# Six value products in one step, expert conversions behind the exp, and a later start of the second batch's scores

## The chip, the cores and the metric

The kernel runs on one core of a Trainium2 chip. The metric is the device time in microseconds of one execution. Before the change the median of three runs is 1456.61 us (1449.06 to 1458.63).

## The reference

The program is an attention block with mixed heads, followed by a bilinear expert layer; everything is float32 (the expert weights arrive as float64 and are rounded on the chip).

```python
# q, k, v: (8, 12, 448, 64), w_pre and w_post: (12, 12)
scores = np.matmul(q, k.transpose(0, 1, 3, 2)) / 8
scores = np.einsum('bhij,hg->bgij', scores, w_pre)
attn = np.exp(scores - np.max(scores, axis=-1, keepdims=True))
attn = attn / (np.sum(attn, axis=-1, keepdims=True) + 1e-09)
attn = np.einsum('bhij,hg->bgij', attn, w_post)
x = np.matmul(attn, v)             # regrouped to (3584, 768)
# w1, w2: (768, 1024), w3: (1024, 1024), w_out: (1024, 768)
out = ((x @ w1) * (x @ w2) @ w3) @ w_out
```

## The kernel before

The scores of a batch are cut into 45 tiles of ten query rows. The main loop in `run` has one **step** n per tile (8 x 45, and six more), and works on tiles in sets m of two. An even step 2m fetches rows of raw scores for a later set, takes the row maxima of set m on DVE (`largest`, L226), and its exp on ACT (`exp`, L234). The odd step 2m+1 scales the second mixing matrix by the sums (`scale`, L243 to L246), multiplies the set before with it on PE (`post`, L259), and mixes the heads of the next set's scores (`mix`, L219). The mix writes the two banks that the exp reads, so it waits for the exp of the set before. Everything is written in program order; each engine, and SP, which issues all DMAs, works through its own instructions in that order.

Around this, the steps carry other work:

- **Scores.** `qk` (L173) makes one unit of raw scores, copies it out of score banks 0 and 1 on ACT (L178, L179), and the next step stores it to DRAM. Lists `qks` and `loads` say in which step a unit is made and its `kq` pair is loaded (six steps ahead). The first batch's units stand in steps 0 to 14.
- **Value products.** After each group of 15 tiles `av` (L300) multiplies six pairs of heads with v, three into one bank. Three pairs are done in an odd step, the other three two steps later, all in bank 0. A copy on ACT (L321, for the first two batches followed by a subtraction on DVE, L322) or a copy and a store (L307) empties it. With a batch's last group the next batch's six v tiles are asked for (`load_v`, L285). The first six are loaded in steps 6 to 11.
- **Conversions.** The float64 expert weights are brought in as words (L100), squared on ACT (L106), put together on DVE in four operations (L116 to L120), and cut into a high part (ACT, L125) and a low part (POOL, L126). `converting` asks for words two conversions ahead. Forty of them (`fold_pieces`) feed the product of w3 and w_out (`folding`, L359, up to step 47); then 32 (`unit_pieces`) make the weights of the experts, which are also stored (L424). One is made in a step at most, and none in a step that has value products.
- **Experts.** The matrix products of the expert layer are handed out as single matmuls by `advance`, so many per step as `shares` works out: it gives more to steps with less other work (a value product counts 5.1, an odd step 9.3, a score unit 3.7).

`self.later`, `self.ends` and `self.soon` are lists of things to issue: at the start of the next step, when `do_ends` is called (after products, to empty banks), and after the maxima. `bank(i, ...)` first issues what still empties bank i.

## Time and profile before

| | |
|---|---|
| median of 3 runs | 1456.61 us |
| profiled execution, its own time | 1456.61 us |
| its span | 1454.8 us |
| PE busy | 1390.1 us, 96% of the span |
| ACT busy | 833.1 us, 57% |
| DVE busy | 739.0 us, 51% |
| POOL busy | 620.7 us, 43% |
| DMA | 416.86 MB, mean 287 GB/s |
| mean granted TensorE clock | 0.985 |

PE is the only engine that is busy nearly all the time. Its busy time includes matmuls that run at a lower granted clock. How busy the others are on the average says little, since the stretches of the program differ: at the start it converts and loads, from about 1280 us on it only runs experts. So the places where PE is idle are what is read, and for each the instruction it waited for.

### The profile page before, as it was taken

The page shows a single profiled execution, that of the slowest core. Times are in us where ns is not written, and L with a number is a line of the kernel's source. Part 1 is how long each engine was busy: PE and PEld are TensorE (multiplying, and loading weights), DVE is VectorE, ACT ScalarE, POOL GpSimd, SP SyncE. Part 2 cuts the span into 40 slices and gives each one's busy share as a digit, 9 for nine tenths or more (in the row PEclk, how much of TensorE's full clock was granted, in tenths as well). Part 3 has the DMA queues.
Part 4 walks back from the last instruction along what each step waited for, and adds up shares of the span by engine and source line. Part 5 has one row for each costly group of instructions (what it writes and reads, how often), then busy time and mean ns, then how long its engine had stood idle before and what let it go on. Part 6 is the DMA issues. An engine that isn't in the chain of part 4 may idle for free.

```text
span 1454.8 us, 45722 instructions
## 1 busy us (share of the span) xinstructions
PE 1390.1 (96%) x18684; PEld 1059.4 (73%) x18684; DVE 739.0 (51%) x1497; ACT 833.1 (57%) x1952; POOL 620.7 (43%) x754
## 2 busy tenths in 40 slices
PE   5789998999999989999999999999999999999998
PEld 2357785776677667776777777777776777899988
DVE  4867565767644544432344445334444447334563
ACT  3876665777756656665555656656655546422231
POOL 1333232444324434632244445444335446446683
PEclk7989998999999999999999999999999999999999
DMA  8998789999999999999989988799879766698875
GB/s 256 365 319 274 237 267 287 311 336 307 316 288 353 348 343 319 368 338 314 311 266 291 319 278 280 234 312 350 288 230 285 236 179 214 206 332 263 240 229 173
DMA packets 203760, 416.86 MB, mean 287 GB/s; under 512 B 20528, under 2 KB 120112, under 8 KB 203472
## 3 DMA queue, kind: packets, MB, share of 16 engines
q1 hardware_dynamic: 203552, 413.94, 87.2%
q8 instruction: 149, 2.44, 0.7%
q14 instruction: 59, 0.48, 0.1%
HBM read 279.77 MB, written 134.09 MB: 284 GB/s over the span
## 4 chain that ended last, share of the span: by engine, by line
PE 78%; DMA 13%; DVE 5%; ACT 3%; issue 1%; SPq 0%; POOL 0%; DVEq 0%; ACTq 0%; POOLq 0%
PE e L701 20%; PE psa L300 10%; PE pso L259 10%; PE psm L219 8%; PE psq L173 7%; PE psf L359 5%; PE eg L521 4%; PE e2o L701 4%; PE e1o L701 4%; PE e3o L701 4%; DMA s_d<-s 3%; PE eo L552 3%; DMA cs<-wo 3%; DMA r<-raw_d 2%; DMA wu<-w_d 2%; ACT e L234 1%
## 5 line engine op out<-in xcount | busy, mean ns | idle before, releaser
L246 POOL TENSOR_SCALAR w<-wpo,ri 128x60 f32<-128x60 f32 x360 | 180.7, 518 | 489.0 <-DVE ri L244 465.8
L226 DVE TENSOR_REDUCE mn<-psm 128x1 f32<-128x448 f32 x360 | 207.8, 619 | 317.0 <-PE psm L219 316.6
L701 PE MATMUL e<-eh,wu 128*128 128x448 f32 x1008 | 297.3, 372 | 6.3 <-DVE c L655 3.2
L273 ACT COPY mt<-pso 128x480 f32<-128x480 f32 x352 | 197.8, 621 | 177.3 <-PE pso L259 177.1
L234 ACT ACTIVATE e<-psm,mn 128x448 f32<-128x448 f32 x360 | 226.6, 642 | 9.6 <-DVE mn L226 9.6
L219 PE MATMUL psm<-r,wsc 60*64 60x448 f32 (+1 forms) x1440 | 197.9, 557 | 32.1 <-ACT e L234 19.9
L701 PEld LDWEIGHTS e<-eh,wu 128*128 128x128 f32 x1008 | 188.0, 188 | 52.5 <-issue 27.4
L259 PEld LDWEIGHTS pso<-w,e 60*64 60x64 f32 x10080 | 174.5, 134 | 50.0 <-issue 44.0
L259 PE MATMUL pso<-w,e 60*64 60x60 f32 x10080 | 198.6, 224 | 0.1
L701 PE MATMUL e<-el,wu 128*128 128x448 f32 x504 | 187.1, 371 | 0.0
L173 PE MATMUL psq<-kq 64*64 64x448 f32 x1176 | 159.5, 546 | 0.6 <-ACT st L178 0.6
L300 PE MATMUL psa<-mt,v 128*64 128x150 f32 (+1 forms) x2304 | 156.9, 293 | 1.9 <-ACT st L178 1.9
L300 PEld LDWEIGHTS psa<-mt,v 128*64 128x64 f32 x2304 | 143.6, 137 | 17.9 <-issue 6.3
L655 DVE TENSOR_TENSOR c<-c,e 128x448 f32<-128x448 f32 x168 | 101.8, 618 | 87.6 <-PE e L701 82.8
L178 ACT COPY st<-psq 128x448 f32<-128x448 f32 x162 | 86.4, 533 | 68.8 <-ACT mt L273 32.8
L521 PE MATMUL eg<-xh,wu 128*128 128x448 f32 x384 | 118.8, 380 | 4.8 <-DMA wu<-w_d 4.8
L640 POOL TENSOR_TENSOR el<-x,eh 128x448 fp32r<-128x448 f32 x90 | 104.2, 1176 | 34.8 <-ACT eh L639 34.8
L701 PEld LDWEIGHTS e<-el,wu 128*128 128x128 f32 x504 | 94.9, 188 | 22.4 <-issue 14.1
L243 DVE TENSOR_SCALAR sa<-sm 128x2 f32<-128x2 f32 x180 | 35.9, 200 | 129.6 <-ACT e L234 129.0
L173 PEld LDWEIGHTS psq<-kq 64*64 64x64 f32 x1176 | 62.2, 136 | 53.8 <-issue 29.8
L521 PEld LDWEIGHTS eg<-xh,wu 128*128 128x128 f32 x384 | 71.8, 190 | 38.1 <-issue 25.3
L179 ACT COPY st<-psq 128x448 f32<-128x448 f32 x162 | 87.7, 541 | 0.0
(99 smaller groups left out, 2011.5 us busy)
## 6 DMA issues: line engine op xcount, KB each, us to landing
r<-raw_d SPq DMA_DIRECT2D x344, 210.0 KB, 4.9
raw_d<-st SPq DMA_DIRECT2D x138, 448.0 KB, 5.4
wu<-w_d SPq DMA_DIRECT2D x104, 384.0 KB, 6.4
wu<-s_d SPq DMA_DIRECT2D x96, 384.0 KB, 4.8
wu<-w_d SPq DMA_DIRECT2D x51, 512.0 KB, 5.6
kq<-kq SPq DMA_DIRECT2D x42, 448.0 KB, 6.2
wu<-s_d SPq DMA_DIRECT2D x36, 512.0 KB, 4.9
x<-x_d SPq DMA_DIRECT2D x72, 224.0 KB, 6.3
```

The lines of the kernel that those rows point to most:

```text
L173: nc.tensor.matmul(ps[s][z * PP:(z + 1) * PP], t[rows, q:q + PP], t[rows, k:k + S], start=True, stop=True)
L219: nc.tensor.matmul(ps[s][c * PP:(c + 1) * PP, :S], self.wsc[k], r[k, c], start=True, stop=True)
L226: self.nc.vector.tensor_reduce(mn[:, s:s + 1], self.psm[m][s][:, :S], axis=AX.X, op=ALU.min)
L234: nc.scalar.activation(e, p[:, :S], AF.Exp, bias=mn[:, s:s + 1], scale=-1.0, accum_out=sm[:, s:s + 1])
L246: nc.gpsimd.tensor_scalar_mul(w2[:, s], self.wpo, ri[:, s:s + 1])
L259: nc.tensor.matmul(self.pso[c][z * PP:(z + 1) * PP, at:at + HK], e[k, j * PP:(j + 1) * PP], w2s[k, s], start=True, stop=True)
L273: self.nc.scalar.copy(dst.rearrange("p j g (s i) -> p j s g i", s=2), src)
L300: nc.tensor.matmul(self.psa[rows, g % 3, :W], v[:, j, rows], mt[:, j, 2 * g + s, :W], start=(j == 0), stop=(j == NJ - 1))
L521: nc.tensor.matmul(p, u[:, k % (K1 // 2), x], xs[y][:, k], start=(k == 0 and t == 0), stop=(k == K1 - 1 and t == 2))
L640: nc.gpsimd.tensor_tensor(lo, x, hi.bitcast(F32), op=ALU.subtract)
L655: nc.vector.tensor_tensor(a[out], a[to[0]], p, op=ALU.add)
L701: nc.tensor.matmul(p, w[:, k, x], ops[m, k][y], start=(k == 0 and t == 0), stop=(k == nk - 1 and t == 2))
```

## The change

Four things change. All six pairs of a group are multiplied in one step (pairs 0 to 2 into bank 0, 3 to 5 into bank 1), the step in which three were before. The expert conversions (`unit_pieces`) are issued later within a step: in an even step behind the exp, in an odd step at its end; they are now also made in the step that lost its three value products. The second batch's score units start at step 14 and not 11, one in 1.3 steps, and its kq loads with them; the first v loads stand in steps 11 to 16. And the experts of the first batch start one step earlier (`E_AT`).

```diff
--- before.py
+++ after.py
@@ -292,7 +292,7 @@
         nc, cols = self.nc, self.cols(a)
         W = cols.stop - cols.start
         if g % 3 == 0:
-            self.psa = self.bank(0, f"psa{b}_{a}_{g}")[:, :3 * GB * IB].rearrange("p (g i) -> p g i", g=3)
+            self.psa = self.bank(g // 3, f"psa{b}_{a}_{g}")[:, :3 * GB * IB].rearrange("p (g i) -> p g i", g=3)
         v, mt = self.vs[b, g], self.mt[b, a]
         for j in range(NJ):
             for s in range(2):
@@ -311,15 +311,15 @@
                 nc.sync.dma_start(dst, x)
                 self.x_made[b] += 1
 
-            self.ends.append((0, leave))
+            self.ends.append((g // 3, leave))
         elif g % 3 == 2:
             if b not in self.xs:
                 pool = self.xp[b % 2]
                 self.xs[b] = [pool.tile([128, K1, S], F32R, tag=f"x{t}", name=f"x{t}{b}") for t in "hl"]
             h, l = (x[:, g - 2:g + 1, cols] for x in self.xs[b])
             q = self.psa[:, :, :W]
-            self.ends.append((0, lambda: nc.scalar.copy(h, q)))
-            self.soon.append((0, lambda: nc.vector.tensor_tensor(l, q, h.bitcast(F32), op=ALU.subtract)))
+            self.ends.append((g // 3, lambda: nc.scalar.copy(h, q)))
+            self.soon.append((g // 3, lambda: nc.vector.tensor_tensor(l, q, h.bitcast(F32), op=ALU.subtract)))
         if a == NG - 1:
             self.later.append(self.load_v)
 
@@ -805,7 +805,7 @@
         for n, u in enumerate([(0, p, c) for c in (1, 2) for p in range(HP)] + [(0, p, 3) for p in range(1, HP, 2)]):
             qks[n] = [u]
         for b in range(1, B):
-            first, per = (11, 28 / 21) if b == 1 else ((b - 1) * NB - 6, NB / 21)
+            first, per = (14, 1.3) if b == 1 else ((b - 1) * NB - 6, NB / 21)
             units = [(b, p, c) for g in range(0, HP, 2) for p, c in [*itertools.product((g, g + 1), range(3)), (g + 1, 3)]]
             for i, (b, p, c) in enumerate(units):
                 n = int(first + i * per) | (b > 1)
@@ -815,11 +815,10 @@
         for b in range(B):
             for a in range(NG):
                 for g in range(HP):
-                    n = (b * NB + (a + 1) * GB + 3) | 1
-                    avs.setdefault(n if g < 3 else n + 2, []).append((b, a, g))
+                    avs.setdefault((b * NB + (a + 1) * GB + 3) | 1, []).append((b, a, g))
 
         N = B * NB
-        FOLD, SWITCH, E_AT = 18, NB + 5, NB + 8
+        FOLD, SWITCH, E_AT = 18, NB + 5, NB + 7
         PAIR, P_AT = 4 * NB + 7, 4 * NB + 15
         P_1 = 7 * 3 * (2 * K1 // 2 * KF // 2 + KF // 2 * K1 // 2)
         E_1, E_2 = 2 * KF * K1 * 3, K1 * KF * 3
@@ -926,7 +925,7 @@
             self.do_later()
             if n + 3 < HP:
                 others(n + 3)
-            elif HP <= n < 2 * HP:
+            elif HP <= n - 5 < 2 * HP:
                 self.load_v()
             for x in loads.get(n, []):
                 self.load_kq(*x)
@@ -948,7 +947,11 @@
             self.do_soon()
             if pieces:
                 next(pieces)
-            elif unit_pieces and not fold_pieces and not avs.get(n):
+
+            def convert():
+                nonlocal unit_pieces, n_pieces, third
+                if pieces or not unit_pieces or fold_pieces or avs.get(n):
+                    return
                 ahead = 1 if n < SWITCH else 2 * done // (3 * K1) + 4 + (done > 0)
                 if n_pieces < ahead:
                     n_pieces += 1
@@ -957,6 +960,7 @@
                     else:
                         next(unit_pieces)
                         third = True
+
             now = share.get(n, 0)
             if n < SWITCH:
 
@@ -966,8 +970,10 @@
 
             advance(now // 2)
             self.do_ends()
-            if not odd and m < SETS:
-                self.exp(m)
+            if not odd:
+                if m < SETS:
+                    self.exp(m)
+                convert()
             advance(now - now // 2)
             for x in avs.get(n, []):
                 self.av(*x)
@@ -979,6 +985,8 @@
             self.do_ends()
             for i, x in enumerate(qks.get(n, [])):
                 self.later.append(self.qk(*x, (6, 7) if i else (0, 1)))
+            if odd:
+                convert()
             if third:
                 next(unit_pieces)
```

How the order of instructions moves is seen at three places.

ACT, the program's steps 53 and 54 before. `cm` is a conversion's Square, `wu` its high part, `e` the exp, `mt` the copies behind `post`.

```order
L106 ACTIVATE cm_3275<-cs_3135 128x384
L273 COPY mt_0_2975<-pso_141 128x4x2x12x5
L273 COPY mt_0_2975<-pso_142 128x4x2x12x5
L125 CAST wu_3323<-cx_3255 128x3x128
L106 ACTIVATE cm_3335<-cs_3247 128x384
L234 ACTIVATE e_0_3349,sm_3348<-psm_0_3315,mn_3330 128x448
L234 ACTIVATE e_1_3351,sm_3348<-psm_1_3316,mn_3330 128x448
L125 CAST wu_3358<-cx_3281 128x3x128
L106 ACTIVATE cm_3373<-cs_3273 128x384
```

The same stretch with the change, from the copies of step 53 on:

```order
L273 COPY mt_0_2966<-pso_141 128x4x2x12x5
L273 COPY mt_0_2966<-pso_142 128x4x2x12x5
L106 ACTIVATE cm_3339<-cs_3239 128x384
L125 CAST wu_3347<-cx_3280 128x3x128
L234 ACTIVATE e_0_3363,sm_3362<-psm_0_3329,mn_3354 128x448
L234 ACTIVATE e_1_3365,sm_3362<-psm_1_3330,mn_3354 128x448
L106 ACTIVATE cm_3369<-cs_3272 128x384
L527 COPY ea_0_3381<-eg_0_0_3261 128x448
L125 CAST wu_3385<-cx_3345 128x3x128
```

In step 54 the Square (the second of the three before, the second of the two after) stood ahead of the two exps and now stands behind them. In step 53 it stood ahead of the copies behind `post` and now stands behind them.

SP, from step 5 to step 8 before. `cs` are a conversion's words, `raw_d<-st` a unit's scores, `r` the rows for the mix, `v` and `kq` the loads that move.

```order
L156 DMA kq_0_472<-kq 128x896
L100 DMA cs_474<-wo 128x768
L201 DMA r_541<-raw_d 60x2x448 x2
L187 DMA raw_d<-st_5_1_538 128x896
L285 DMA v_0_545<-v 128x512
L100 DMA cs_547<-wo 128x768
L187 DMA raw_d<-st_0_2_576 128x896
L285 DMA v_1_580<-v 128x512
L100 DMA cs_582<-wo 128x768
L201 DMA r_649<-raw_d 60x2x448 x2
L187 DMA raw_d<-st_1_2_646 128x896
L285 DMA v_2_653<-v 128x512
```

With the change:

```order
L100 DMA cs_472<-wo 128x768
L201 DMA r_539<-raw_d 60x2x448 x2
L187 DMA raw_d<-st_5_1_536 128x896
L100 DMA cs_543<-wo 128x768
L187 DMA raw_d<-st_0_2_572 128x896
L100 DMA cs_576<-wo 128x768
L201 DMA r_643<-raw_d 60x2x448 x2
L187 DMA raw_d<-st_1_2_640 128x896
L156 DMA kq_0_647<-kq 128x896
L100 DMA cs_649<-wo 128x768
L187 DMA raw_d<-st_2_2_678 128x896
L100 DMA cs_682<-wo 128x768
```

Three v loads and the kq load are gone from among the words, rows and stores here; the kq load now stands in step 8 and the v loads begin in step 11.

PE, the last group of the first batch, before: step 49, from the last fold matmuls to the first of `post`, and step 51, from the last scores on.

```order
L359 MATMUL psf_7_2940<-fo,fw_2678 128x384 x19
L300 MATMUL psa_2_0_3039<-mt_2_2168,v_0_545 64x148 x8
L300 MATMUL psa_2_0_3039<-mt_2_2168,v_1_580 64x148 x8
L300 MATMUL psa_2_0_3039<-mt_2_2168,v_2_653 64x148 x8
L259 MATMUL pso_141<-w_2922,e_0_2905 64x60
L259 MATMUL pso_142<-w_2922,e_0_2905 64x60
```

```order
L173 MATMUL psq_1_2_1_3103<-kq_1_2471 64x448
L300 MATMUL psa_2_3_3161<-mt_2_2168,v_3_688 64x148 x8
L300 MATMUL psa_2_3_3161<-mt_2_2168,v_4_765 64x148 x8
L300 MATMUL psa_2_3_3161<-mt_2_2168,v_5_799 64x148 x8
L259 MATMUL pso_141<-w_3033,e_0_3012 64x60
```

With the change, step 49:

```order
L359 MATMUL psf_7_2930<-fo,fw_2681 128x384 x18
L300 MATMUL psa_2_0_3039<-mt_2_2178,v_0_787 64x148 x8
L300 MATMUL psa_2_0_3039<-mt_2_2178,v_1_859 64x148 x8
L300 MATMUL psa_2_0_3039<-mt_2_2178,v_2_892 64x148 x8
L300 MATMUL psa_2_3_3064<-mt_2_2178,v_3_963 64x148 x8
L300 MATMUL psa_2_3_3064<-mt_2_2178,v_4_1006 64x148 x8
L300 MATMUL psa_2_3_3064<-mt_2_2178,v_5_1080 64x148 x8
L259 MATMUL pso_141<-w_2923,e_0_2904 64x60
L259 MATMUL pso_142<-w_2923,e_0_2904 64x60
L259 MATMUL pso_141<-w_2923,e_0_2904 64x60
```

The three products of step 51 now follow those of step 49, in a bank of their own.

## Rows read from the trace of the kernel before

**Rows 1.** The page's first part, of the whole span: busy us (share) and instructions

```profile
PE 1390.1 (96%) x18684; PEld 1059.4 (73%) x18684; DVE 739.0 (51%) x1497; ACT 833.1 (57%) x1952; POOL 620.7 (43%) x754
```

**Rows 2.** By stretch: engines' busy us, granted clock, DMA share, GB/s

```profile
46.14:92.47 46.33, 33.40 (x531) 17.37 (x523) 36.73 (x73) 37.38 (x89) 18.79 (x24) 0.93 1.03 368
92.47:214.44 121.97, 120.70 (x1651) 94.51 (x1655) 79.40 (x165) 80.67 (x194) 37.01 (x53) 0.99 0.82 259
214.44:262.66 48.22, 41.42 (x670) 29.08 (x664) 27.93 (x62) 30.75 (x75) 13.43 (x19) 0.89 0.93 300
262.66:403.45 140.79, 137.21 (x2195) 97.77 (x2189) 96.10 (x202) 105.12 (x253) 57.97 (x80) 1.00 0.95 315
403.45:720.00 316.55, 305.55 (x4610) 225.71 (x4604) 133.15 (x286) 196.42 (x465) 125.03 (x156) 0.99 0.99 334
720.00:1281.50 561.50, 556.29 (x8035) 430.88 (x8031) 252.59 (x538) 318.94 (x750) 251.66 (x320) 1.00 0.83 262
```

**Rows 3.** PE's waits over the span: us in total, times, longest us

```profile
PE psm L219 <- ACT e L234: 19.9, 15, 5.8
PE psm L219 <- DMA r<-raw_d: 11.1, 2, 8.9
PE psa L300 <- ACT st L178: 1.9, 3, 0.7
```

**Rows 4.** Timeline near 239 us: start, us, instruction, idle before, releaser

```profile
234.91 0.70 SPq L100 DMA_DIRECT2D cs<-w  x1
243.62 0.56 ACT L106 ACTIVATE cm<-cs 128x384 f32<-128x384 f32 x1 [6.84 <-DMA cs<-w]
244.83 2.38 PE L219 MATMUL psm<-r,wsc 60*64 60x448 f32 x8 [5.83 <-ACT e L234]
```

**Rows 5.** Busy us of each engine, granted clock, DMA, from 240 to 255 us

```profile
240.00:255.00 15.00, 10.17 (x100) 5.98 (x101) 8.40 (x19) 8.79 (x21) 4.13 (x6) 0.66 0.89 287
```

**Rows 6.** DMA issues over the span: xcount, KB each, median us to landing

```profile
r<-raw_d SPq DMA_DIRECT2D x344, 210.0 KB, 4.9
raw_d<-st SPq DMA_DIRECT2D x138, 448.0 KB, 5.4
kq<-kq SPq DMA_DIRECT2D x42, 448.0 KB, 6.2
v<-v SPq DMA_DIRECT2D x48, 256.0 KB, 5.3
```

**Rows 7.** The chain that ended last, 36 to 116 us: start us, us, what

```profile
65.57 8.33 DMA cs<-wo
```

**Rows 8.** The page's groups of instructions: busy us, mean ns, idle before

```profile
L173 PE MATMUL psq<-kq 64*64 64x448 f32 x1176 | 159.5, 546 | 0.6 <-ACT st L178 0.6
L300 PE MATMUL psa<-mt,v 128*64 128x150 f32 (+1 forms) x2304 | 156.9, 293 | 1.9 <-ACT st L178 1.9
```

**Rows 9.** DVE: tile ca's instructions in a stretch (four a conversion), then groups

```profile
0.00:400.00 400.00, 169.25 (x288) 0.95 0.91 298
L226 DVE TENSOR_REDUCE mn<-psm 128x1 f32<-128x448 f32 x360 | 207.8, 619 | 317.0 <-PE psm L219 316.6
L243 DVE TENSOR_SCALAR sa<-sm 128x2 f32<-128x2 f32 x180 | 35.9, 200 | 129.6 <-ACT e L234 129.0
L244 DVE RECIPROCAL ri<-sa 128x2 f32<-128x2 f32 x180 | 29.9, 166 | 15.4 <-DVE sa L243 0.5
```

**Rows 10.** Timeline of PE, the score mix of steps 57 and 59

```profile
252.91 0.98 PE L219 MATMUL psm<-r,wsc 60*64 60x448 f32 x7
257.89 0.98 PE L219 MATMUL psm<-r,wsc 60*64 60x448 f32 x7
```

**Rows 11.** Timeline of ACT and PE, the waits near 311 and 382 us

```profile
311.18 1.22 PE L219 MATMUL psm<-r,wsc 60*64 60x448 f32 x5 [1.35 <-ACT e L234]
381.20 0.55 ACT L106 ACTIVATE cm<-cs 128x384 f32<-128x384 f32 x1 [2.40 <-DMA cs<-w]
382.42 0.96 PE L219 MATMUL psm<-r,wsc 60*64 60x448 f32 x2 [1.76 <-ACT e L234]
```

## The prediction

> **What bounds the kernel now.** I read the page's first part, then PE by stretches, then who ended PE's waits, then the places of those waits. The profiled execution took 1456.61 us, which is also the median of the three runs; its span is 1454.8 us, so 1.8 us lie around it. PE is busy 1390.1 us of the span [rows 1], so 64.7 us are idle, and nothing that leaves PE's own work as it is can win more than that and what the half clock costs. The change neither adds nor removes arithmetic. So the question is which idle time goes, and what takes its place.
>
> The stretches [rows 2] are cut where the score mixes (L219) of steps 5, 17, 47, 61 and 107 start. From 46.14 to 92.47 us PE is busy 33.4 of 46.3 us while the DMA engines are full (share 1.03, 368 GB/s) and DVE is busy 36.7. From 92.47 to 214.44 PE is full: 120.7 of 122.0. From 214.44 to 262.66 it loses 6.8 us and part of the clock (0.89). From 262.66 to 403.45 it loses 3.6, from 403.45 to 720 11.0 with the DMA engines full (0.99), and from 720 to 1281.5, where the last scores end, 5.2. The list of PE's waits [rows 3] says what: most is L219 waiting for the exp on ACT, 19.9 us in 15 waits.
>
> The largest of those, 5.8 us, is read from the timeline [rows 4]. The conversion of step 54 stands ahead of the exp on ACT. Its words were issued at 234.91, its Square (L106) starts only at 243.62 after 6.84 us of waiting for that DMA, the exp (L234) follows, and PE's L219 starts at 244.83, 5.83 us late. The clock pays too [rows 5]: from 240 to 255 us the grant is 0.66 on the mean, which is 10.2 of the 15 us at the 1.2 GHz level. Of these PE worked about 6.4 (from 244.83 on), which at 2.4 GHz would have been 3.2. The Trainium skill, "TensorE: Matmul & The Clock Gate", section Terms, counts the throttled time times one minus the ratio, 5.1 us here; the rows give 3.2, since PE stood still for the rest.
>
> **The change part by part.**
>
> *Early loads and scores (steps 5 to 17).* The six loads of v move from steps 6 to 11 to steps 11 to 16, the second batch's kq loads and score units start three steps later. The last conversion of this stretch waits for words issued in step 15. Ahead of them the queue now has one v load (256 KB), one kq load (448 KB) and two raw stores (448 KB each) fewer [rows 6]: 1600 KB, 1.64 MB, at 368 GB/s 4.5 us. The chain of waits crosses the stretch's later half on such words, three times, the longest 8.33 us [rows 7], so I take the 4.5. The ends: 2.5 us if all bytes issued by step 17 count (896 KB fewer), and 9.6 if DVE's busy time (46.3 less 36.7) is the floor. Two score units now fall into the next stretch, where PE is full. A unit is eight of the 1176 instructions of L173 [rows 8], 159.5/147 = 1.09 us, so 2.2 come back. Net **-2.3 us** (ends -0.3 and -7.4). The v loads still stand three steps ahead of their first use in step 19.
>
> *All six pairs in one step.* One av call is 16 instructions of L300 [rows 8], 156.9/144 = 1.09 us. Three calls move two steps ahead, from a step on PE to another; the sum on PE stays. PE waits three times for a copy out of the score bank before a first product [rows 3]; of the three places the one in step 21 (and that in step 51, counted below) goes, step 33 stays: **-0.6 us** (ends 0 and -0.6). The second bank's copy and subtraction are issued behind the first's and have the post product and mix in front of the next scores as cover; without it the scores would wait for one more copy in 24 places, at most the 0.7 us that the longest such wait takes in rows 3.
>
> *Conversions behind the exp (steps 47 to 61).* In even steps Square now stands behind the exp on ACT, so late words hold back only casts and copies that PE needs one or two steps later. The 6.8 us of idle time [rows 2] and the 3.2 of clock, 10.0 together, lose their cause. But the DVE part does not move between its neighbours: the four ops of a conversion in an odd step still stand ahead of the next row maximum. A conversion is 169.25/72 = 2.35 us of DVE [rows 9]. A pair of steps with two of them has 4.70 of conversion, two maxima of 0.62, and 0.20 and 0.17 of scaling [rows 9], 6.3 us in a chain, while PE turns a full pair in 4.98 (L219 at 252.91 and 257.89, [rows 10]). With three value products gone from step 51, the change converts in every step from 50 to 56, so three pairs run at DVE's pace: 3 x 1.3 = 4.0 us of new idle time. I take **-6.0 us** (ends 0, if the wait is only passed on to DVE, and -10.0).
>
> *Later conversions (steps 62 to 100).* The same wait costs 1.76 us at 382.42, where Square waited 2.40 us for words. At 311.18, 1.35 us, it is DVE that was late: a conversion in odd step 77 ran ahead of the maximum [rows 11]. In the change step 98 has its conversion behind the exp, and step 77 has none (76 and 78 have). **-3.1 us** (ends 0 and -3.6, all idle time of that stretch).
>
> *What the DMA engines give back.* From 214.44 to 403.45 they moved 300 x 48.2 and 315 x 140.8, 58.8 MB in 189.0 us. In 9.1 us less that is 327 GB/s, close to the 334 of the next stretch, where PE idles 11.0 of 316.6 us, 3.5%. At that share it would be 6.3 us; I take a third, **+2.0 us** (ends 0 and +6.3), since 327 is below 334 and the early stretch moved 368. The queue order on SP is otherwise the same: a step's words stand behind its loads before and after. The experts' start one step earlier moves some eight matmuls of PE work forward and adds none. Behind 403 us I count 0, with ends of 4 either way.
>
> The sum is -2.3 - 0.6 - 6.0 - 3.1 + 2.0 = -10.0 us, so 1456.6 becomes **1446.6 us**.
>
> **The rivals.**
> - *Nothing takes the place of the waits.* DVE makes its conversions while PE has other work. Then the terms are -2.3, -0.6, -10.0, -3.1 and no return, 16.0 us: 1440.6. For it: what held PE in rows 4 was words, and not DVE's own work. Against: seven conversions in seven steps.
> - *The queue is the bound.* What is won up to 403 us meets a stretch with full DMA engines, and PE waits there instead: 9.1 us come back, and 2.9 stay, 1453.7. For it: share 0.99 over 316 us [rows 2]. Against: those engines moved 334 GB/s there and 368 earlier. The Trainium skill, "DMA: Bandwidth & Descriptors", section Specifications, gives about 358 GB/s of HBM for a core; by that rule (an estimate) the early stretch with 368 was at the limit and the later one 7% below it, and the trace agrees that the early one is where the engines held up the chain.
> - *Six loads of v at once, slower.* From the second batch on the loads of v stand in one piece of six where they were three and three. 1536 KB at 334 GB/s are 4.7 us ahead of the next rows r, which land in 4.9 us by themselves [rows 6]; they are asked for two pairs of steps ahead, 10 us by rows 10. When the sum, 9.6, passes that, L219 waits. The trace has one such wait behind the start, 2.2 us (11.1 less 8.9, [rows 3]); with 3.2 of clock as in rows 5 that is 5.4. In the three bursts that fall where the engines are nearly full (steps 94, 140 and 184) 16.2 us: 1462.8, slower than before.
>
> **How the numbers follow.** The forecast 0.52, nothing in place of the waits 0.22, the queue 0.17, six loads 0.06, something else 0.03. The range takes in the forecast's bounds that are likely together, and the first three cases: with the early term at its far end and the first rival 1435, with the queue giving all back and 4 us more behind it 1459. What a measurement of this kernel can tell from no change is about 1%, 14.6 us, so faster means under 1442.0 and slower over 1471.2. Faster: two thirds of the first rival (0.15) and the forecast's lower part (0.13), 0.28. Slower: half of the six loads, 0.03. Within 1%: 0.69.
>
> **What would show it.** On ACT, exp ahead of Square in even steps and no wait of PE for the exp over 2 us between 214 and 262; the clock at full level there. On DVE, busy nearly without a gap through steps 50 to 56: if PE has no idle time there, the first rival is right. In the early stretch, the mix of step 17 some 4.5 us earlier, at about 88; if it is at 92 still, the loads that moved were not what the words waited behind. Between 403 and 720 PE's idle time near 11 us; 18 and more would be the queue. Waits of L219 for r right behind steps 140 and 184 would be the six loads. The forecast is wrong if the sum of PE's idle time over the span does not fall by 5 us or more.

## The result, and the profile after

The change made the kernel slower by a little: a median of 1461.97 us (1456.04 to 1468.68, 20 runs) against 1456.82 us before (1449.06 to 1464.09, 20 runs), a ratio of 1.0037 with a 95% interval of 1.0020 to 1.0055. The forecast was 1446.6. The profiled execution took 1468.68 us, the highest of its 20 and 6.7 us over their median, so of its rows I argue from those that other kernels' traces repeat.

The page's first part after the change (busy us, share of the span, instructions):

```profile
PE 1399.1 (95%) x18684; PEld 1063.4 (72%) x18684; DVE 747.5 (51%) x1497; ACT 834.2 (57%) x1952; POOL 620.0 (42%) x754
```

Against [rows 1] PE is busy 9.0 us longer with the same instructions, and in a span of 1466.9 us it is idle 67.8 us, not 64.7. The stretches, cut at the mixes (L219) of the same steps as [rows 2]; the fifth ends at the mix of step 201:

```profile
46.03:89.16 43.13, 31.52 (x514) 17.73 (x506) 37.18 (x72) 35.63 (x85) 18.79 (x24) 0.88 0.99 344
89.16:213.68 124.52, 122.79 (x1672) 93.97 (x1672) 78.04 (x165) 82.66 (x197) 36.37 (x53) 1.00 0.85 272
213.68:260.49 46.81, 43.28 (x677) 30.42 (x670) 34.91 (x66) 32.62 (x79) 15.39 (x21) 0.96 0.92 312
260.49:404.78 144.29, 138.61 (x2187) 98.18 (x2181) 97.74 (x198) 103.62 (x249) 54.78 (x78) 0.98 0.92 310
404.78:728.68 323.90, 310.81 (x4670) 229.27 (x4666) 134.63 (x286) 197.16 (x466) 122.94 (x154) 0.98 0.95 324
```

The first four pieces took 46.33, 121.97, 48.22 and 140.79 us before, so they go -3.2, +2.6, -1.4 and +3.5. The fifth (steps 107 to 201) took 317.8 us before, from 403.45 to 721.25, and is 6.1 longer now. The rest, from step 201 on, is 4.7 longer. The loss stands behind 403 us, where I had counted nothing. The traces of three kernels below that also have six products in one step there repeat the fifth piece (six_only 324.6, six_mid 322.2, after_v33 324.2 us), and those that keep three and three there have it shorter (312.9 to 318.7 us in the kernel before, later_only, convert_only and, up to step 186, six_not_mid). The 4.7 us of the rest they don't repeat: after_v33 takes 733.6 us there, as the kernel before does. In the fifth piece the DMA engines are also no longer full: 0.95 and 324 GB/s, against 0.99 and 334 in [rows 2]. The 104.9 MB of this stretch (324 x 323.9) would take 314.2 us at 334 GB/s; 9.7 us of DMA are missing.

PE's waits over the span (us in total, times, longest), which answer to [rows 3]:

```profile
PE psm L219 <- ACT e L234: 14.3, 11, 4.6
PE psm L219 <- DMA r<-raw_d: 14.0, 5, 8.8
PE psq L173 <- ACT st L178: 10.5, 6, 5.4
PE eg L521 <- DMA wu<-w_d: 5.9, 4, 2.3
...
PE psa L300 <- ACT st L178: 1.7, 2, 1.1
```

The waits for the exp fell by 5.6 us. The waits for r went from two to five.

What happens at a step with six products shows on SP. Steps 121 to 123, first the changed kernel (start, us, instruction):

```profile
453.81 0.34 SPq L562 DMA_DIRECT2D out<-eos  x1
454.20 0.45 SPq L156 DMA_DIRECT2D kq<-kq  x1
461.07 0.80 SPq L201 DMA_DIRECT2D r<-raw_d  x2
461.96 1.22 SPq L311 DMA_DIRECT2D x_d<-xd  x2
```

Then the kernel before, at the same place:

```profile
452.67 0.33 SPq L156 DMA_DIRECT2D kq<-kq  x1
456.37 0.80 SPq L201 DMA_DIRECT2D r<-raw_d  x2
457.26 0.55 SPq L311 DMA_DIRECT2D x_d<-xd  x1
```

The fetch of step 124 (L201) writes the buffer of r that the mix of step 123 reads. There are two such buffers, so SP waits at the fetch until that mix is done, and everything behind it waits too. The mix starts at 460.02 in the changed kernel and at 455.32 in the one before. So after the kq load SP issues nothing for 6.4 us (454.65 to 461.07), where it was 3.4. What that does to the DMA engines, by pairs of steps (us, then each engine's busy us, granted clock, DMA share, GB/s); the changed kernel, steps 121 to 123 and 123 to 125:

```profile
448.79:460.02 11.23, 11.23 (x192) 9.52 (x187) 5.04 (x8) 4.84 (x11) 2.68 (x3) 1.00 0.98 364
460.02:465.42 5.40, 5.40 (x97) 3.82 (x93) 1.47 (x3) 4.71 (x11) 2.02 (x2) 1.00 0.66 180
```

The kernel before, the same steps:

```profile
447.12:455.32 8.20, 8.20 (x145) 6.46 (x139) 5.04 (x8) 4.30 (x10) 2.68 (x3) 1.00 1.04 370
455.32:463.69 8.37, 8.37 (x144) 6.65 (x140) 2.75 (x5) 5.41 (x12) 4.53 (x5) 1.00 1.03 379
```

PE works without a gap in both, 16.63 us and 16.57. But 8.2 + 8.4 became 11.2 + 5.4, and in the short pair the DMA engines have run dry: 0.66 and 180 GB/s. As a measure for other kernels I sum, over each microsecond between the mixes of steps 107 and 201, what the share is short of 1. This **unused DMA time** is 11.4 us before and 24.3 after.

The time is paid later, in stalls, and behind the four longest of the stretch comes a lower clock. Which dry pair leads to which stall is not shown; that the hold is behind the total, the runs with a third buffer show below. At 593 us PE waits for a unit of expert weights (`wu`; timeline, with the idle time before and its releaser):

```profile
593.09 0.74 PE L521 MATMUL eg<-xh,wu 128*128 128x448 f32 x1 [1.92 <-DMA wu<-w_d]
```

Four places of the stretch, all right behind stalls of 1.6 to 2.4 us (for wu, wu, the exp and r), with the granted clock in the third column from the end:

```profile
528.24:531.65 3.41, 3.11 (x8) 2.81 (x9) 0.00 (x0) 0.35 (x1) 0.00 (x0) 0.50 0.99 373
593.09:596.50 3.41, 3.41 (x9) 3.06 (x10) 1.34 (x4) 0.86 (x4) 2.49 (x4) 0.50 1.00 365
644.29:647.70 3.41, 3.41 (x17) 1.16 (x15) 1.49 (x4) 1.02 (x4) 0.83 (x2) 0.50 1.04 377
695.49:698.90 3.41, 3.10 (x15) 0.87 (x14) 0.80 (x2) 0.00 (x0) 0.00 (x0) 0.50 1.06 367
```

At 0.50, the 1.2 GHz level, 13.0 us of PE's work cost 6.5 more than at 2.4. Before there was one such place in the stretch, of 3.41 us, where PE was busy throughout, so 1.7 us. Not every stall of this length is followed by one: the kernel before waits 2.24 us for r until 689.65 us and goes on at full clock (1.00):

```profile
689.65:697.12 7.47, 6.84 (x85) 4.28 (x89) 1.49 (x4) 2.74 (x7) 0.84 (x2) 1.00 1.03 358
```

Of the 6.1 us that the stretch is longer, PE is busy for 4.0 (310.8 us against 306.8 with the same 4670 instructions) and idle for 2.1. The busy part is about what the clock costs, 6.5 less 1.7 by these rows, since busy time counts slow matmuls as busy. The Trainium skill, "TensorE: Matmul & The Clock Gate", section Terms, takes the throttled time times one minus the ratio, 6.8 us for these 13.64. Here the trace agrees (6.5), since PE hardly stood still in them.

### The profile page after: what moved, and what is told of

Read it like the earlier page. It is cut to its first block, busy times and chain, and to the rows that moved or that the text cites. A ratio compares the mean times of both kernels' runs of the same rounds, so it can differ in the third digit from the quotient of the medians.

```text
span 1466.9 us, 45752 instructions
## 1 busy us (share of the span) xinstructions
PE 1399.1 (95%) x18684; PEld 1063.4 (72%) x18684; DVE 747.5 (51%) x1497; ACT 834.2 (57%) x1952; POOL 620.0 (42%) x754
## 4 chain that ended last, share of the span: by engine, by line
PE 79%; DMA 13%; DVE 4%; ACT 2%; issue 1%; SPq 0%; POOL 0%; DVEq 0%; ACTq 0%; POOLq 0%
PE e L701 19%; PE psa L300 10%; PE pso L259 10%; PE psm L219 9%; PE psq L173 7%; PE eg L521 6%; PE psf L359 4%; PE e2o L701 4%; PE e3o L701 4%; PE e1o L701 3%; PE eo L552 3%; DMA wu<-w_d 2%; DMA cs<-wo 2%; DMA r<-raw_d 2%; DMA wu<-s_d 2%; DMA s_d<-s 1%
## 5 line engine op out<-in xcount | busy, mean ns | idle before, releaser
L219 PE MATMUL psm<-r,wsc 60*64 60x448 f32 (+1 forms) x1440 | 201.1, 559 | 29.7 <-ACT e L234 14.3
L173 PE MATMUL psq<-kq 64*64 64x448 f32 x1176 | 163.8, 553 | 0.6 <-ACT st L178 0.6
L300 PE MATMUL psa<-mt,v 128*64 128x150 f32 (+1 forms) x2304 | 151.6, 291 | 1.7 <-ACT st L178 1.7
L243 DVE TENSOR_SCALAR sa<-sm 128x2 f32<-128x2 f32 x180 | 45.2, 251 | 125.0 <-ACT e L234 124.4
L521 PEld LDWEIGHTS eg<-xh,wu 128*128 128x128 f32 x384 | 73.8, 195 | 38.4 <-issue 22.5
```

The lines of the kernel that those rows point to most:

```text
L173: nc.tensor.matmul(ps[s][z * PP:(z + 1) * PP], t[rows, q:q + PP], t[rows, k:k + S], start=True, stop=True)
L219: nc.tensor.matmul(ps[s][c * PP:(c + 1) * PP, :S], self.wsc[k], r[k, c], start=True, stop=True)
L300: nc.tensor.matmul(self.psa[rows, g % 3, :W], v[:, j, rows], mt[:, j, 2 * g + s, :W], start=(j == 0), stop=(j == NJ - 1))
L521: nc.tensor.matmul(p, u[:, k % (K1 // 2), x], xs[y][:, k], start=(k == 0 and t == 0), stop=(k == K1 - 1 and t == 2))
```

## Experiments

Ratios are to the kernel before, in the same series on the same chip (its medians 1455.2, 1457.2, 1455.0, 1453.9 and 1454.8 us), with 95% intervals.

### Which part costs

**six_only**: the kernel before with the new place of the products, their banks and `E_AT`; the six v tiles are then asked for at once as well. Of its edit, one line:

```diff
-                    avs.setdefault(n if g < 3 else n + 2, []).append((b, a, g))
+                    avs.setdefault((b * NB + (a + 1) * GB + 3) | 1, []).append((b, a, g))
```

> The kernel before with one part of the change alone: all six value products in one step over two banks, the experts one step earlier; the six loads of v fall into one step with it. Theory V (six loads of v at once make words, rows and units land late, and the clock drops behind each stall): slower than before by 5 to 10 us, 1462 to 1467, with stalls of PE some four steps behind the bursts of steps 94, 140, 274. Theory S (the uneven steps themselves cost): the same time, but stalls at any place. Theory C (the conversions' new place costs): no slower than before, 1457. Forecast's view, that none of it costs: 1455 to 1457.

Measured: 1463.78 us, ratio 1.0063 (1.0039 to 1.0087); unused DMA time 23.5. The whole loss is in this part. Which of the things in it costs, the next runs say.

**convert_only**: only the conversions' new place.

```diff
-            elif unit_pieces and not fold_pieces and not avs.get(n):
...
+                convert()
```

> The kernel before with the expert conversions at the end of a step alone. The forecast's term for it: the 5.8 us wait near 239 us, its clock and the 1.8 us wait near 382 go, 6 to 10 us less, 1447 to 1451. Theory C (DVE or ACT wait for the words in the new place instead): 1455 to 1462. Theories V and S say nothing against a gain here.

Measured: 1455.98 us, ratio 1.0002 (0.9978 to 1.0027), so a gain of 6 to 10 us, as forecast, is excluded. The stretches of steps 47 to 61 and 61 to 107 in its trace:

```profile
216.09:262.04 45.95, 41.25 (x670) 28.78 (x664) 33.16 (x64) 31.42 (x77) 13.40 (x19) 0.96 0.98 319
262.04:404.49 142.45, 138.68 (x2195) 98.04 (x2189) 97.05 (x200) 105.04 (x252) 57.09 (x80) 1.00 0.94 313
```

188.4 us against 189.0 in [rows 2]. The idle time of PE fell, from 10.4 to 8.5 us, and hardly the length.

**later_only**: only the later loads and scores of the second batch.

```diff
-            first, per = (11, 28 / 21) if b == 1 else ((b - 1) * NB - 6, NB / 21)
+            first, per = (14, 1.3) if b == 1 else ((b - 1) * NB - 6, NB / 21)
...
-            elif HP <= n < 2 * HP:
+            elif HP <= n - 5 < 2 * HP:
```

> The kernel before with the second batch's scores and the first loads of v later, alone. The forecast's term: -2.3 us, 1454.5. The traces of before and after differ by -0.6 us up to step 47, which would be no measurable difference, 1456. If the wait of 5.4 us near 74 us in the trace of the change belongs to this part, 1457 to 1460.

Measured: 1455.26 us, ratio 0.9995 (0.9971 to 1.0019): no difference that can be told from none, nor from the 2.3 us that were forecast.

**after_v33**: the changed kernel, with the loads of v three and three, two steps apart.

```diff
-            self.later.append(self.load_v)
+            (self.later if g < 3 else self.late).append(self.load_v if g < 3 else (self.step + 3, self.load_v))
```

> The changed kernel, but the six loads of v of a batch's end are issued three and three, two steps apart, as before; the products stay in one step. Theory V: the stalls four steps behind the bursts go, 1450 to 1455, that is 7 to 12 us less than the changed kernel. Theory S: no difference from the changed kernel, 1460 to 1463. Theory C: the same, 1460 to 1463.

Measured: 1461.03 us, ratio 1.0041 (1.0017 to 1.0064), unused DMA time 23.7. The burst of six loads isn't the cause.

### Where it costs

**six_mid** and **six_not_mid**: six_only with the six products in one step only inside, or only outside, of steps 107 to 186. Six_mid leaves `E_AT` as it was. Its edit:

```diff
-                    avs.setdefault((b * NB + (a + 1) * GB + 3) | 1, []).append((b, a, g))
+                    n = (b * NB + (a + 1) * GB + 3) | 1
+                    avs.setdefault(n if g < 3 or LATE <= n < 4 * NB + 7 else n + 2, []).append((b, a, g))
```

> The kernel before, with six products in one step only for the six groups of steps 109 to 183 (batches 2 and 3), where the DMA engines are full; the other 18 groups stay three and three. Theory S (a long pair of steps holds SP at the next fetch, nothing new is asked for, the DMA queue runs dry, and in a stretch that is full that time is not made up): about the whole loss of six_only, ratio 1.004 to 1.007, 1461 to 1465 us, and in the trace the DMA time lost between steps 107 and 201 near 23 us where the kernel before has 11. Rival P (each long step costs the same, wherever it stands): 6 of 24 groups, a quarter of the loss, ratio 1.001 to 1.002, about 1457.5.

> The complement: six products in one step for the 18 groups outside of steps 109 to 183, three and three inside. Theory S: as before, ratio 0.999 to 1.002, about 1456, DMA time lost in steps 107 to 201 near 11 us. Rival P: three quarters of the loss, ratio 1.004 to 1.006, about 1462.

Measured: 1459.43 us, 1.0024 (1.0000 to 1.0049), for the six groups inside; 1458.95 us, 1.0014 (0.9996 to 1.0032), for the 18 outside. Unused DMA time 22.8 and 13.7, as theory S had it, and 22.8 without the experts' earlier start. In time six_not_mid is where theory S put it (0.999 to 1.002), and its interval leaves out rival P's 1.004. Six_mid settles nothing: its interval reaches into both ranges. By the middles a group inside costs 0.0004 and one outside 0.00008, but the two losses add up to less than six_only's, and I take no more from it than that the full stretch holds more than its share of groups.

### Taking the hold away

**six_r3** and **before_r3**: a third buffer for r, so that the fetch waits for an older mix.

```diff
-        r = self.rp.tile([128, 2, S], F32, tag="r", name=f"r{m}", bufs=2)
+        r = self.rp.tile([128, 2, S], F32, tag="r", name=f"r{m}", bufs=3)
```

> six_only with three buffers in place of two for the rows r, nothing else. The fetch of an even step then waits for the mix of three steps earlier, not for the one just before it, so a long step doesn't hold SP. Theory S: the queue no longer runs dry behind a long step, DMA time lost in steps 107 to 201 falls from 23 to 15 or less, and at least half of the loss comes back: 1457 to 1460 against 1463.8 of six_only. Rival: SP is held by other things (the experts' weight buffers, stores that wait for ACT), or it is PE's own work in the long step that costs; then six_r3 is at 1462 to 1465 like six_only.

> The control: the kernel before with three buffers for r. Theory S: its steps are even and the queue seldom runs dry, so little is won, ratio 0.997 to 1.001, 1451 to 1457. If SP's wait at the fetch cost the kernel before as well, it gains more, 1446 to 1451, and then the third buffer is a gain of its own and six_r3 must be compared with this run.

Measured: six_r3 1442.16 us, 0.9900 (0.9878 to 0.9923); before_r3 1445.06 us, 0.9919 (0.9895 to 0.9942). Unused DMA time 10.9 and 6.1. The gain is far larger than theory S said, since the kernel before paid for the hold as well. And six products in one step cost nothing any more: 0.9900/0.9919 = 0.9981, within 0.003, where with two buffers they cost 1.0063; the two differ by 0.8%, within 0.4.

**after_r3**, **no_six_r3**, **after_r3_w4**: the same third buffer in the changed kernel; in the changed kernel with its products three and three; and in the changed kernel with the units of expert weights asked for four ahead.

```diff
-        self.loaded, self.n_loaded, self.n_asked, self.w_ahead = [], 0, 0, 3
+        self.loaded, self.n_loaded, self.n_asked, self.w_ahead = [], 0, 0, 4
```

> The changed kernel with three buffers for r and nothing else. Theory S (the change's loss is SP held at the fetch behind long steps): the loss goes with the hold, so it is no slower than before_r3 (1445.1) and near six_r3 (1442.2): 1438 to 1446, ratio 0.988 to 0.993. Rival: the change has a cost of its own beside SP's hold (conversions packed on DVE, words behind the six loads); then it stays 5 us over before_r3, 1449 to 1453.

> Three buffers for r, the conversions at their new place and the later start of the second batch's scores, value products three and three. Against before_r3 it has the two parts that alone gave nothing, against after_r3 it lacks the six products. If those two parts were held back by the queue, as the forecast's rival of a bound queue said, they gain now: 1437 to 1441. If their gain is eaten by PE's own waits within the steps (DVE's row maxima behind conversions), nothing changes: 1443 to 1447.

> after_r3 with the experts' units asked for four ahead in place of three while batches run singly (the pool has five buffers). The waits of the expert products for their units (L521 for wu, 5.9 us in 4 waits of the changed kernel) should go. Theory S: with SP free the queue is deep enough and it adds little, 0 to 3 us less than after_r3. Rival: the units come late because they are asked for late; then 4 to 8 us less.

Measured: after_r3 **1438.25 us, 0.9886 (0.9853 to 0.9918)**; no_six_r3 1444.51 us, 0.9925 (0.9902 to 0.9949); after_r3_w4 1438.40 us, 0.9889 (0.9855 to 0.9924). The loss goes with the hold, and the changed kernel with the third buffer beats the changed kernel and the kernel before. The two parts that gave nothing alone give nothing here either (no_six_r3 stands at before_r3), so it wasn't a full queue that ate their gain. Units asked for earlier add nothing.

SP's waits say what the buffer did (us in total, times, longest; L201 is the fetch of r, L392 the load of expert weights, L187 the store of raw scores, L311 that of value products). Over the span, the first of the changed kernel:

```profile
SPq L201 <- PE psm L219: 300.4, 97, 8.5
SPq L392 <- PE e L701: 80.5, 66, 3.2
```

The kernel before has this row as well:

```profile
SPq L201 <- PE psm L219: 310.4, 110, 6.4
```

In sum it is no longer with the change. In steps 107 to 201 the same row reads, first with the change, then before:

```profile
SPq L201 <- PE psm L219: 57.4, 19, 7.8
SPq L201 <- PE psm L219: 50.4, 21, 4.8
```

And after_r3, over the span:

```profile
SPq L187 <- ACT st L179: 183.1, 73, 6.9
SPq L392 <- PE e L701: 136.6, 101, 3.4
...
SPq L201 <- PE psm L219: 1.9, 3, 0.9
```

Of the 300 us of waiting for the mix, the longest 8.5, there are 1.9 left. SP now waits elsewhere, for ACT's copies. At steps 121 to 123 it goes on through the long pair: the fetch is issued at 446.82 and two stores follow within 3.0 us from 449.03, the first ahead of the mix at 451.65, and the pair behind it moves 297 GB/s and not 180:

```profile
446.82 1.96 SPq L201 DMA_DIRECT2D r<-raw_d  x2
449.03 2.97 SPq L311 DMA_DIRECT2D x_d<-xd  x2
```

```profile
440.40:451.65 11.25, 11.25 (x191) 9.59 (x187) 5.04 (x8) 4.84 (x11) 2.67 (x3) 1.00 1.03 375
451.65:457.06 5.41, 5.41 (x99) 3.83 (x93) 1.48 (x3) 4.71 (x11) 2.03 (x2) 1.00 0.97 297
```

The stretch of steps 107 to 201 has full DMA engines again and is 11.1 us shorter than in the changed kernel:

```profile
396.88:709.64 312.76, 303.93 (x4670) 226.90 (x4666) 134.26 (x286) 197.42 (x466) 123.57 (x154) 0.99 1.00 338
```

### Another way past the hold

**after_fetch_late**, **before_fetch_late**, **six_fetch_late**, **after_r3_fetch_late**: the fetch of an even step behind the step's other DMAs on SP, in the changed kernel, the kernel before, six_only and after_r3.

```diff
-            if not odd and LF <= n + LF < N:
-                self.fetch(m + LF // 2)
             self.do_later()
...
             for x in loads.get(n, []):
                 self.load_kq(*x)
+            if not odd and LF <= n + LF < N:
+                self.fetch(m + LF // 2)
```

> The changed kernel, two buffers for r, with the fetch of an even step moved on SP behind the step's units, stores and loads of v and kq (it stood ahead of them). SP is held at the fetch as before, but those others no longer stand behind it. If the loss is what stands behind the fetch (units, stores), a part comes back: 1455 to 1459. If it is that SP is held at all and the rows themselves and all of the next step come late, nothing or worse: 1461 to 1468.

> The control for after_fetch_late: the kernel before, with the fetch of an even step behind the step's units, stores and loads on SP. Theory S (what the hold costs is what the long steps of the change add): before has even steps, its hold costs less, so it gains less than the 8.6 us of the changed kernel: 1450 to 1457. Rival: the order is better for any step length; then it gains as much, 1446 to 1449, and six products in one step still cost 5 us or more beside it.

> six_only with the fetch behind the step's other DMAs on SP. before_fetch_late was at ratio 1.0026 with three and three, six_only at 1.0063 with the fetch ahead. Theory S (six in one step costs only while SP is held behind the mix): 0.998 to 1.003, 1452 to 1459, no slower than before_fetch_late. Rival (the conversions' new place made the 8.6 us that the later fetch won in the changed kernel, and six costs as before): 1.006 to 1.010, 1463 to 1468.

> Third buffer for r and the later fetch together, on the changed kernel. If both take away one and the same hold, nothing is added: 1436 to 1441, as after_r3 (1438.3). If the later fetch also makes the rows r later against the mix, it is slower than after_r3: 1441 to 1446. If what stands behind the fetch is still held with three buffers, 1432 to 1436.

Measured: after_fetch_late 1453.37 us, 0.9992 (0.9972 to 1.0013), better than forecast; before_fetch_late 1458.01 us, 1.0026 (1.0012 to 1.0041); six_fetch_late 1458.79 us, 1.0019 (1.0005 to 1.0033); after_r3_fetch_late 1454.98 us, 0.9997 (0.9982 to 1.0013). So the order isn't better by itself: it costs the kernel before 0.3% and takes the third buffer's gain away. What it does is to put another hold in the place of the mix, the same one with two buffers and with three. After_fetch_late's SP:

```profile
SPq L187 <- ACT st L179: 252.6, 103, 7.8
...
SPq L201 <- PE psm L219: 42.4, 23, 4.1
```

The stores stand ahead of the fetch now, and SP waits at them for ACT. In after_r3_fetch_late the same wait is 244.8 us, and PE waits for r 15 times, 11.6 us in all. In both ways in which SP is hardly held at the mix, six in one step costs nothing that can be measured (0.9900 against 0.9919 above, 1.0019 against 1.0026 here).

### The next hold

**after_st_act** and **after_r3_st_act**: the stores of raw scores of batches 2 to 7 issued by ACT, with two and three buffers for r. **after_r3_stores_late**: with three, the stores of batches 1 to 7 later on SP, behind the step's units, loads and words.

```diff
-        return lambda: nc.sync.dma_start(raw[c * QT:c * QT + n, 2 * p:2 * p + 2], st[:n])
+        return lambda: (nc.sync if b < 2 else nc.scalar).dma_start(raw[c * QT:c * QT + n, 2 * p:2 * p + 2], st[:n])
```

```diff
-                self.later.append(self.qk(*x, (6, 7) if i else (0, 1)))
+                (self.later if x[0] < 2 else self.stores).append(self.qk(*x, (6, 7) if i else (0, 1)))
```

> The changed kernel, two buffers for r, with the stores of raw scores of batches 2 to 7 issued by ACT, right behind the copies they wait for, and not by SP. SP's waits at L187 for ACT go (most of 65 us), the hold at the fetch stays. Theory S (the hold at the fetch behind long steps is the loss): little changes, 1457 to 1463. Rival (any hold of SP costs alike, the stores' too): 1452 to 1457.

> The same stores issued by ACT, with three buffers for r. There SP is held longest at these stores (183 us in 73 waits). If a hold costs wherever it is, as the fetch's did, 1428 to 1434 against 1438.3 of after_r3. If the queue is deep enough once the fetch is free, so that this hold is hidden, 1436 to 1441; with ACT's time for issuing on the path of the exp, more.

> after_r3 (ratio 0.9886) with the stores of raw scores of batches 1 to 7 one step's work later on SP, behind the step's loads, units and words, so that SP's wait for the copies on ACT (183 us in 73 waits) holds nothing that could already go. If this hold costs as the fetch's did, 0.983 to 0.987, 1430 to 1436. If the queue is deep enough by now, 0.987 to 0.991. If the later stores make the copies on ACT wait for their buffers, slower, 0.991 to 0.995.

Measured: after_st_act 1498.32 us, 1.0290 (1.0265 to 1.0315); after_r3_st_act 1494.12 us, 1.0276 (1.0251 to 1.0302): above every range I gave, and told in the last section. After_r3_stores_late 1441.72 us, 0.9894 (0.9873 to 0.9915), like after_r3. SP still waits 182.3 us at L187, so the run moved this wait behind other transfers and didn't take it away; it says that what stood behind the wait in after_r3 cost nothing that can be measured.

### The products in one step and the hold, together

| ratio to before | fetch ahead, two buffers | three buffers | fetch later |
|---|---|---|---|
| three and three | 1 | 0.9919 | 1.0026 |
| six in one step | 1.0063 | 0.9900 | 1.0019 |
| the whole change | 1.0037 | 0.9886 | 0.9992 |

Down the columns the change costs 0.37% in the first. In the others it is at 0.9886/0.9919 = 0.9967 (within 0.004, the intervals' halves added in squares), which can't be told from 1, and 0.9992/1.0026 = 0.9966 (within 0.003).

## Why the prediction was wrong

The step that failed is **"All six pairs in one step"**: "Three calls move two steps ahead, from a step on PE to another; the sum on PE stays", sized at -0.6 us, and with it "Behind 403 us I count 0, with ends of 4 either way". The sum on PE does stay. But a pair of steps grew from 8.2 to 11.2 us, and I didn't ask who waits for the end of a step: SP, at the next fetch. I had written that "the queue order on SP is otherwise the same"; it is, but not the times at which SP may go on. Six_only says that the term is +9.2 us (0.0063 x 1455; 5.7 to 12.7), and six_r3 against before_r3 that it goes away with the hold. SP's list of waits in the trace of the kernel before has the hold as its first row, 310.4 us in 110 waits. I read the list of PE, not that of SP.

*Early loads and scores.* Right in kind. The mix of step 17 came at 89.16 us, 3.3 earlier; 4.5 was expected. Over nine traces with the later start steps 5 to 17 are 4.5 us shorter on the mean than over nine with the old one, as forecast (the two kernels whose stores ACT issues are left out here and below). Behind them 3.0 come back and not 2.2: steps 5 to 47 take 167.1 us and 168.6, -1.5, where I had -2.3.

*Conversions.* Right in where the wait goes, wrong in size. PE's waits for the exp over 2 us between 214 and 262 us went from 5.8 to one of 2.2. From the mix of step 49 to that of step 57 DVE is busy 21.70 of 24.80 us and PE is idle for 3.5 of them, near the 4.0 that I had counted for DVE's pace:

```profile
225.72:250.52 24.80, 21.27 (x325) 13.24 (x320) 21.70 (x41) 17.56 (x42) 9.50 (x12) 0.93 0.92 309
```

So the first rival (nothing takes their place) is wrong as well. Over nine traces each, steps 47 to 107 take 190.4 us with the conversions at the old place (186.5 to 193.2) and 188.2 at the new one (184.6 to 192.5): -2.2 us, where the terms -6.0, -3.1 and +2.0 gave -7.1. Even that is too much, since more of the second nine have the third buffer; among those with two buffers and the fetch ahead it is -1.8, among those with three -1.0, within a spread of several us, and convert_only's time shows no gain. Two things were mis-sized. The 10 us of [rows 4, 5] are the largest of nine cases: idle time and clock together, the nine traces with the old place lose 7.9 us on the mean in steps 47 to 61 (6.2 to 10.0), those with the new one 6.2 (5.2 to 9.1). And odd steps still have the four DVE operations ahead of the row maximum. At 378 us, behind the six loads of v, that shows (DVE, then PE; idle time before and its releaser):

```profile
377.83 0.36 DVE L116 TENSOR_SCALAR ca<-cs 128x384 int32<-128x384 int32 x1 [5.07 <-DMA cs<-w]
...
380.57 1.14 DVE L226 TENSOR_REDUCE mn<-psm 128x1 f32<-128x448 f32 x2
```

```profile
381.99 1.75 PE L219 MATMUL psm<-r,wsc 60*64 60x448 f32 x5 [4.58 <-ACT e L234]
```

Late words now hold the maxima on DVE, and through them the exp, as they held the exp on ACT in [rows 4].

*The rivals.* "The queue is the bound" named the right engine and the right stretch. Its mechanism, that the queue gives back what was won ahead of it, is not what happened: it couldn't make the kernel slower, and six_only, with nothing won ahead, loses no less. What failed was not the DMA engines' speed but that they had nothing to do: the mean of 324 GB/s after the change holds pairs at 364 and at 180. The Trainium skill, "DMA: Bandwidth & Descriptors", section Specifications, whose 358 GB/s for a core I had put beside this rival, doesn't mark a limit in these rows: pairs moved 364, 370 and 379. "Six loads of v at once" had the sign and a time near the result (1462.8), by luck: after_v33 shows that it is not the cause, and the mark I gave for it is absent, since the only mix in the stretch that waits for r is that of step 193, in the changed kernel (2.4 us) as in the kernel before (2.2).

*What would show it.* The forecast was to be wrong if PE's idle time over the span didn't fall by 5 us; it rose by 3.1. I had also said that 18 us and more of idle time between 403 and 720 us would be the queue. It is 13.1 for the same steps, and the clock's share, which I hadn't counted in that mark, is the larger part of the loss. The upper end of the range, 1459, isn't the sum given for it either: 1453.7 and 4 are 1457.7.

What stays open: how much of the six products' cost falls outside of steps 107 to 186, and whether the changed kernel is ahead by some 0.3% where SP is hardly held at the mix. With the third buffer that can't be told from nothing, with the later fetch it is just clear of it, and the parts show no gain each by itself.

## What to carry to other kernels

Where, as here, one engine issues all transfers in order, a transfer that must wait for a buffer holds every later one. What the change added doesn't show in the sum of these waits over the span (300.4 us against 310.4) but in the long ones (up to 8.5 us against 6.4), behind which the DMA engines run dry. Before work is gathered in one step, read the issuing engine's list of waits, and ask for its first row which step ends it. A third buffer for that one tile (3.5 KB of each partition) was worth more than the change: -0.8% on the kernel before, -1.1% with the change.

## What the runs showed of the hardware that was not expected

In steps 107 to 201 of the changed kernel four stalls of PE of 1.6 to 2.4 us were each followed by 3.41 us at the 1.2 GHz level, and the kernel before has one of 2.24 us that was not (rows above). Six_only and after have 25.5 and 22.5 us of loss at that level over the span, the kernel before 16.5, after_r3 11.9 (worked out as half of PE's busy time there, in one execution each). The time doesn't follow it from kernel to kernel: six_not_mid has 26.2 at a ratio of 1.0014.

The stores moved to ACT cost 2.5% of the changed kernel (1.0290 against 1.0037) and 3.9% of after_r3 (1.0276 against 0.9886). ACT then stands at a store whose data it has made itself. After_r3_st_act, ACT, SP and PE near 490 us:

```profile
483.26 0.54 ACT L179 COPY st<-psq 128x448 f32<-128x448 f32 x1
490.02 1.53 ACTq L184 DMA_DIRECT2D raw_d<-st  x2
491.59 0.63 ACT L234 ACTIVATE e<-psm,mn 128x448 f32<-128x448 f32 x1 [7.79 <-DMA wu<-w_d]
```

```profile
484.14 1.48 SPq L201 DMA_DIRECT2D r<-raw_d  x2
```

```profile
492.37 1.63 PE L219 MATMUL psm<-r,wsc 60*64 60x448 f32 x4 [5.67 <-ACT e L234]
```

The copy ended at 483.80, the store was issued 6.2 us later, the exp stood behind it, and PE behind the exp; PE's waits for the exp are 45.5 us in 22 over the span, where after_r3 has 7.8 in 11, and the loss at the lower clock is 32.9 us against 11.9. What held the store is in the trace's semaphores. All DMAs of this program, SP's and ACT's, signal their landing on the same eight, and before it issues the store ACT waits for the one that the store itself will use. Here that is the semaphore of the second of SP's two fetches above, issued at 485.21; it landed at 489.94, and 0.1 us later the store went. Of the 36 waits of over 0.3 us that ACT has at these stores, 31 are for such an earlier transfer, 29 of them for one of SP's; they are 78 of 80 us. The Trainium skill, "DMA: Bandwidth & Descriptors", section "Issuing engines are not separate DMA queues", says that issuing from several engines saves only the issue time; here it cost 2.5 and 3.9%, and the second issuer is one that PE waits for.
